# Moving the scaling of the float64 weights' lower words from VectorE to ScalarE

## The chip, the cores and the metric

The kernel runs on one core of a Trainium2 chip. The metric is the device time of one execution in microseconds, the median of several runs. Times inside an execution come from a hardware profile of one run; they count from the first instruction, and the distance from the first to the last instruction is called the span.

## The reference

Three layers follow one another: windowed attention (four heads plain, four dilated), a gated linear layer, and a soft mixture of experts. All arithmetic is on 2,304 tokens of 512 numbers.

```python
# attention: q, k, v are (4, 8, 576, 64); each row sees a window of 32 keys (heads 4-7: every 4th of 128)
scores = np.where(masks, scale * q @ k.T, -1e9)
attn = softmax(scores);  x = (attn @ v) -> (2304, 512)
# gated layer, w_gate and w_val are (512, 1536), w_out is (1536, 512)
x = (1 / (1 + np.exp(-(x @ w_gate))) * (x @ w_val)) @ w_out
# soft experts: phi (512, 32), w1 (8, 512, 1024), w2 (8, 1024, 512)
logits = x @ phi
slot_input = softmax(logits, axis=0).T @ x
slot_out = relu(slot_input @ w1) @ w2        # by expert, 4 slots each
out = softmax(logits, axis=1) @ slot_out
```

The inputs q, k, v, w1, w2 and phi are float32. The three weights of the gated layer arrive as float64 (numpy's `/ np.sqrt(...)` makes them so), and the kernel gets their raw 64-bit words. [...]

## The kernel before, in words

**Attention** is cut into 20 units, five token blocks n by four head pairs hp. A unit loads its q and k (line 269) and v (line 276), computes scores on TensorE (tile `s_ps`), a softmax (VectorE reductions and a subtraction, a ScalarE Exp at line 184, a normalization on VectorE in block 0 and on GpSimd in the others, line 189), is turned by TensorE transposes into `tr`, copied by ScalarE to `pt_ring` (line 196), and multiplied with v into `xp` (line 222; for later blocks it lies in the bank of `s_ps`). `finish_unit` splits that result into a high part `x_hi` (ScalarE cast, line 250) and a remainder `x_lo` (VectorE subtraction, line 251).

**The gated layer** runs `l1(n, f, ...)` for a token block n and 12 column groups f. Per f there are two products, gate and value, of 12 matmuls each into a bank `l1ps` (line 470; two banks): high weight by x_hi, high weight by x_lo, low weight by x_hi. ScalarE takes the gate's bank with a Tanh (line 480), VectorE the value's bank (line 456). The weights of an f come as `whl`: `split_w` casts them on ScalarE (line 433) and subtracts on VectorE or GpSimd (line 434). For block 0 and f = 0 to 11 the source of `whl` is the converted tile `fw` itself; in block 1 it is read back from DRAM (`wst`), where it was stored.

**The conversion** is the part that the change touches. `convert(z)` handles 18 tiles: 12 of gate and value weights, two per column group, and six of w_out (the last, by position, is number 17). `stage(z)` loads the raw words into `st` (line 361, one tile ahead, two buffers); `store()` writes an earlier result to DRAM (line 365). The conversion works in two halves of 128x512. For each half, four operations in this order: ScalarE turns the upper word to a scaled float (Prelu, line 379), VectorE shifts it by three bits (line 380), VectorE scales the lower word to a rounded integer (line 381), and GpSimd adds the two (line 382). So there are 36 of each. The first two conversions are written after step `C0 = 21` of block 0's attention, the others with `LA = 2` column groups of lead in the loop over f of block 0, and the six of w_out along block 1. After a w_out tile is converted, `slot_weights` turns and multiplies it on TensorE (line 408, tile `wt_ps`).

**What sets the order.** The program is written without waits. When it is built, a scheduler sets each engine's order: of the instructions that it takes to be ready, at times that it estimates, the one written earliest goes first, with line 480 and 456 preferred (`high_priority`) and with the order of some instructions kept as written (`keep_in_program_order`: most loads, TensorE's attention steps, the later pair products). On the chip each engine runs its own list in that order and stops at the first instruction whose inputs or buffer are not there. SP issues all the transfers that matter here, in one list: loads of q, k and v, `stage`, `store`, and the reloads of weights (line 898). Buffers are reused by tag: `st` has two, `whl` two, `fw` takes turns over four tags for the first 12.

After about 192 us there are no conversions any more: blocks 2 and 3 are computed as a pair, then block 4, and the experts.

Of the kernel before, what the change touches and what calls it, by code (L numbers as in the profile page):

```python
# [10 lines left out]
I32 = mybir.dt.int32  # L11
BF16 = mybir.dt.bfloat16
AF = mybir.ActivationFunctionType
ALU = mybir.AluOpType
# [42 lines left out]
def tile_kernel(  # L57
# [10 lines left out]
    nc = tc.nc  # L68
# [14 lines left out]
    def b8(tag, shape, dt, name):  # L83
        return big.tile(shape, dt, tag=tag, name=name, bufs=BUFS[tag])
# [272 lines left out]
    def stage(z):  # L357
        if z in staged:
            return
        staged[z] = b8("l2", [P, 1024, 2], U32, "st")  # L360
        ld(nc.sync.dma_start(staged[z].rearrange("p a b -> p (a b)"), wd[z].bitcast(U32)))

    def store():
        while stores:
            ld(nc.sync.dma_start(*stores.pop(0)))

    def convert(z):
        i = n_conv[0]
        n_conv[0] += 1
        stage(z)  # L370
        if i + 1 < len(turn):
            stage(turn[i + 1])
        st = staged[z]
        store()
        fw = b8(("ws", "ws", "gb", "xt")[i % 4] if i < NF else ("gb", "xt")[i % 2], [P, 2, 1024], F32, "fw")
        for h in range(2):
            c = slice(512 * h, 512 * h + 512)
            top, low = fw[:, 0, c], fw[:, 1, c]
            nc.scalar.activation(top, st[:, c, 1].bitcast(F32), AF.Prelu, scale=2.0**-112, alpha=2.0**32)  # L379
            nc.vector.tensor_scalar(top.bitcast(U32), top.bitcast(U32), 3, None, ALU.logical_shift_left)  # L380
            nc.vector.tensor_scalar(low.bitcast(I32), st[:, c, 0], 2.0**-29, None, ALU.mult)  # L381
            nc.gpsimd.tensor_tensor(low.bitcast(I32), top.bitcast(I32), low.bitcast(I32), ALU.add)  # L382
        if z < NF:
            stores.append((wg32[z // 2][:, z % 2], fw[:, 1]))
        else:
            y = z - NF
            stores.append((wo32[y // 2][:, 2 * (y % 2) : 2 * (y % 2) + 2].rearrange("p a c -> p (a c)"), fw[:, 1]))
            slot_weights(2 * y, fw[:, 1].rearrange("p (c x) -> p c x", c=2), 3)
        return fw[:, 1]
# [10 lines left out]
    def slot_weights(f, wo_f, lag):  # L400

        wt = pm.rearrange("p a b -> p (a b)").rearrange("p (k c x) -> p k c x", k=ND, c=2)
        at_ = {}

        def turned(c):
            wt_ps = ps_a.tile([P, ND, P], F32, tag="a", name="wt_ps")
            for kc in range(ND):
                nc.tensor.transpose(wt_ps[:, kc], wo_f[:, c, P * kc : P * kc + P], ident)
            nc.scalar.copy(wt[:, :, c], wt_ps)

        def product():
            pt_ps = ps_m.tile([P, 2, P], F32, tag="m", name="pt_ps")
            for kc in range(ND):
                nc.tensor.matmul(
                    pt_ps[32 * kc : 32 * kc + 32], lhsT=phi[:, kc, :], rhs=wt[:, kc], start=True, stop=True
                )
            at_["pt"] = cpool.tile([P, 2, P], F32, tag="pt", name="pt")
            nc.vector.tensor_copy(at_["pt"], pt_ps)

        def summed():  # L420
            wp_ps = ps_m.tile([P, 2, 32], F32, tag="m", name="wp_ps")
            for c in range(2):
                nc.tensor.matmul(wp_ps[:, c], lhsT=at_["pt"][:, c], rhs=i4, start=True, stop=True)
            nc.vector.tensor_scalar(wp[:, f : f + 2], wp_ps, 0.5, None, ALU.mult)

        for n, (step, *args) in enumerate(((turned, 0), (turned, 1), (product,), (summed,))):
            later.append((ticks[0] + lag + n, step, args))
# [453 lines left out]
    def ahead(z):  # L881
        if z < NF:
            conv[z] = convert(z)
# [34 lines left out]
    for f in range(NF):  # L918
        whl = split_w(wst[f // 2][:, f % 2])
        if f % 2:  # L920
            load_w(f // 2 + 2)
        l1(1, f, whl, beside)
        if NF + f in wo_at:
            convert(NF + wo_at[NF + f])
# [97 lines left out]
    for f in range(NF):  # L1022
        c = f % 4
# [255 lines left out]
```

## Time and profile before

| | |
|---|---|
| median of 3 runs | 497.39 us (496.50 to 498.11) |
| the profiled execution, its own time | 496.94 us |
| its span | 495.2 us |
| granted TensorE clock, mean | 0.992 |
| TensorE busy | 468.6 us, 95% of the span |
| VectorE busy | 311.0 us, 63% |
| ScalarE busy | 213.1 us, 43% |
| GpSimd busy | 156.8 us, 32% |

TensorE is busy nearly always, by the pipelined ends that the profile models. The shares are means over stages of different kinds, so they don't say what a change in one stage is worth. The rows below give the stages in which conversions run, and what TensorE waited for in them.

### The profile page before, as it was taken

The numbers are of one execution on the slowest core, as the hardware profiler recorded it, in microseconds if no ns is written. First come the engines' busy times: TensorE is split into PE (matmuls) and PEld (weight loads), VectorE is DVE, ScalarE is ACT, GpSimd is POOL, SyncE is SP. The second block draws the span as 40 slices with busy tenths as digits, with TensorE's granted clock in tenths as the row PEclk, the third lists the DMA queues.
The fourth block names the chain that finished last, engine by engine and source line by source line (L and its number), as shares of the span: only waits on it lengthen the run. The fifth ranks groups of instructions, "written<-read, shape, count | busy, mean of one in ns | idle before, by whom it ended". The sixth has DMA issues, their size and how long they took to land.

```text
span 495.2 us, 12830 instructions
## 1 busy us (share of the span) xinstructions
PE 468.6 (95%) x5488; PEld 357.3 (72%) x5488; DVE 311.0 (63%) x629; ACT 213.1 (43%) x414; POOL 156.8 (32%) x132
## 2 busy tenths in 40 slices
PE   6889999999899998999889999999999999999993
PEld 3558888887788876886557888888887889742552
DVE  3879898758666745436987656655547765541532
ACT  2455645435445534314744554554535343300223
POOL 0244536416445314235154323334212124110100
PEclk9899999999999999999999999999999999999998
DMA  8979978995896079120002201201499886579997
GB/s 301 421 276 361 351 234 306 310 344 195 322 368 253 2 253 394 63 86 1 1 1 86 85 25 61 86 5 80 142 372 422 345 326 259 190 296 367 428 402 239
DMA packets 23785, 112.14 MB, mean 226 GB/s; under 512 B 2352, under 2 KB 7216, under 8 KB 14640
## 3 DMA queue, kind: packets, MB, share of 16 engines
q1 hardware_dynamic: 23408, 111.06, 60.0%
q8 instruction: 43, 0.70, 0.6%
q10 hardware_dynamic: 320, 0.26, 0.2%
q14 instruction: 14, 0.11, 0.1%
HBM read 97.16 MB, written 14.16 MB: 225 GB/s over the span
## 4 chain that ended last, share of the span: by engine, by line
PE 80%; DVE 8%; DMA 4%; ACT 2%; issue 2%; POOL 1%; SPq 1%; DVEq 0%; ACTq 0%
PE l1ps L470 32%; PE pa L592 11%; PE pe L592 6%; PE tp L757 3%; PE s_ps L222 3%; PE h_ps L1045 3%; PE lt_ps L721 3%; PE pd L592 3%; PE s_ps L162 3%; PE so_ps L1104 3%; DMA wo<-fw 2%; PE sp L786 2%; PE tr L195 2%; DMA qk<-qkv 2%; DVE s L556 1%
## 5 line engine op out<-in xcount | busy, mean ns | idle before, releaser
L470 PE MATMUL l1ps<-x_hi,whl 128*128 128x512 f32 x384 | 129.4, 402 | 2.6 <-ACT x_hi L250 2.5
L470 PEld LDWEIGHTS l1ps<-x_hi,whl 128*128 128x128 f32 x384 | 71.7, 188 | 19.0 <-ACT x_hi L250 3.2
L470 PE MATMUL l1ps<-x_lo,whl 128*128 128x512 f32 x192 | 75.6, 394 | 0.0
L382 POOL TENSOR_TENSOR fw<-fw 128x512 int32<-128x512 int32 x36 | 49.0, 1370 | 61.7 <-DVE fw L381 24.7
L470 PEld LDWEIGHTS l1ps<-x_lo,whl 128*128 128x128 f32 x192 | 36.2, 188 | 6.6 <-DVE x_lo L251 0.2
L456 DVE SCALAR_TENSOR_TENSOR g<-g,l1ps 128x512 f32<-128x512 f32 (+1 forms) x36 | 21.4, 594 | 29.3 <-PE l1ps L470 29.0
L470 PE MATMUL l1ps<-x,whl 128*128 128x256 f32 x288 | 37.0, 285 | 0.0
L470 PEld LDWEIGHTS l1ps<-x,whl 128*128 128x128 f32 x288 | 35.4, 192 | 0.4 <-issue 0.2
L480 ACT ACTIVATE g<-l1ps 128x512 f32<-128x512 f32 (+1 forms) x36 | 18.9, 526 | 37.4 <-PE l1ps L470 37.4
L434 POOL TENSOR_TENSOR whl<-w,whl 128x512 fp32r<-128x512 f32 x12 | 15.9, 1326 | 51.2 <-ACT whl L433 39.7
L379 ACT ACTIVATE fw<-st 128x512 f32<-128x512 f32 x36 | 22.8, 675 | 12.4 <-DMA st<-wd 9.2
L757 PE MATMUL tp<-cst,g 128*128 128x128 f32 x216 | 28.0, 275 | 0.0
L757 PEld LDWEIGHTS tp<-cst,g 128*128 128x128 f32 x216 | 24.0, 140 | 5.0 <-issue 3.3
L762 ACT COPY gt<-tp 128x512 f32<-128x512 f32 x27 | 15.6, 584 | 25.0 <-PE tp L757 21.9
L176 DVE TENSOR_REDUCE mx<-s_ps 128x4 f32<-128x256 f32 x40 | 15.2, 413 | 14.3 <-PE s_ps L162 8.4
L380 DVE TENSOR_SCALAR fw<-fw 128x512 uint32<-128x512 uint32 x36 | 22.7, 640 | 1.9 <-ACT fw L379 1.0
L655 DVE TENSOR_TENSOR tm<-pe,tm 128x512 f32<-128x512 f32 x12 | 8.3, 691 | 24.1 <-PE pe L592 24.1
L434 DVE TENSOR_TENSOR whl<-fw,whl 128x512 fp32r<-128x512 f32 x24 | 20.9, 884 | 3.7 <-ACT whl L433 3.2
L381 DVE TENSOR_SCALAR fw<-st 128x512 int32<-128x512 uint32 x36 | 17.8, 528 | 7.7 <-DMA wst<-wg 3.7
L189 POOL TENSOR_TENSOR sm<-sm,su 128x512 f32<-128x512 f32 x12 | 13.6, 1130 | 28.3 <-DVE su L188 26.4
L434 POOL TENSOR_TENSOR whl<-wst,whl 128x512 fp32r<-128x512 f32 x12 | 15.9, 1326 | 19.0 <-ACT whl L433 11.7
L433 ACT CAST whl<-fw 128x512 fp32r<-128x512 f32 x24 | 14.6, 620 | 16.1 <-POOL fw L382 11.7
(455 smaller groups left out, 962.1 us busy)
## 6 DMA issues: line engine op xcount, KB each, us to landing
ew<-w SPq DMA_DIRECT2D x32, 1024.0 KB, 7.8
st<-wd SPq DMA_DIRECT2D x18, 1024.0 KB, 9.1
wst<-wg SPq DMA_DIRECT2D x12, 1024.0 KB, 7.7
v<-qkv SPq DMA_DIRECT2D x20, 512.0 KB, 6.1
wg<-fw SPq DMA_DIRECT2D x12, 512.0 KB, 7.8
w<-wg SPq DMA_DIRECT2D x6, 1024.0 KB, 7.5
qk<-qkv SPq DMA_DIRECT2D x10, 576.0 KB, 5.7
qk<-qkv SPq DMA_DIRECT2D x8, 528.0 KB, 5.5
```

The costliest lines, as they stand in the source:

```text
L176: nc.vector.tensor_reduce(mx[:, 4 * r : 4 * r + 4], u["s_ps"][r], AX.X, ALU.max)
L379: nc.scalar.activation(top, st[:, c, 1].bitcast(F32), AF.Prelu, scale=2.0**-112, alpha=2.0**32)
L380: nc.vector.tensor_scalar(top.bitcast(U32), top.bitcast(U32), 3, None, ALU.logical_shift_left)
L381: nc.vector.tensor_scalar(low.bitcast(I32), st[:, c, 0], 2.0**-29, None, ALU.mult)
L382: nc.gpsimd.tensor_tensor(low.bitcast(I32), top.bitcast(I32), low.bitcast(I32), ALU.add)
L434: (nc.gpsimd if pool[h] else nc.vector).tensor_tensor(whl[:, 1, h], src[:, h], whl[:, 0, h].bitcast(F32), ALU.subtract)
L456: return nc.vector.scalar_tensor_tensor(g, g, 1.0, val, ALU.add, ALU.mult)
L470: nc.tensor.matmul(pt[:, 0:nt], lhsT=whl[:, w_, a, dc, :], rhs=x_[n][:, dc, :], start=first, stop=(dc == HP_ORDER[-1] and w_ == 1),)
L480: nc.scalar.activation(g, pt[:, 0:nt], AF.Tanh, scale=0.5)
L592: nc.tensor.matmul(pt, lhsT=w[:, w_, P * c : P * c + P], rhs=x_[:, c], start=first and c == 0 and w_ == 0 and x_ is hi, stop=c == 1 and w_ ...
L757: nc.tensor.transpose(tp[:, c], g_sb[self.n, 4 * q + c][:, P * j : P * j + P], ident)
L762: nc.scalar.copy(to, tp)
```

## The change

One line in `convert`. The lower words of a half are multiplied by 2 to the power of -29 and written as rounded integers by a ScalarE activation with the function Copy and an immediate scale. Before, a VectorE operation did this. Inputs, output tile, shapes and everything around it are the same.

```diff
             top, low = fw[:, 0, c], fw[:, 1, c]
             nc.scalar.activation(top, st[:, c, 1].bitcast(F32), AF.Prelu, scale=2.0**-112, alpha=2.0**32)
             nc.vector.tensor_scalar(top.bitcast(U32), top.bitcast(U32), 3, None, ALU.logical_shift_left)
-            nc.vector.tensor_scalar(low.bitcast(I32), st[:, c, 0], 2.0**-29, None, ALU.mult)
+            nc.scalar.activation(low.bitcast(I32), st[:, c, 0], AF.Copy, scale=2.0**-29)
             nc.gpsimd.tensor_tensor(low.bitcast(I32), top.bitcast(I32), low.bitcast(I32), ALU.add)
```

## Rows read from the trace of the kernel before

**Rows 1.** Stretches: length, busy us (count) of PE, PEld, DVE, ACT, POOL; clock; DMA

```profile
15.00:36.00 21.00, 16.17 (x427) 11.67 (x426) 16.38 (x39) 12.30 (x25) 8.68 (x6) 0.97 0.91 357
36.00:120.00 84.00, 84.00 (x1161) 68.20 (x1162) 70.24 (x138) 42.71 (x80) 37.38 (x29) 1.00 0.84 296
120.00:192.00 72.00, 69.34 (x1191) 54.94 (x1189) 45.45 (x105) 34.45 (x67) 30.81 (x26) 1.00 0.71 256
```

**Rows 2.** TensorE's waits, 15 to 36 us: us in total, times, longest

```profile
PE l1ps L470 <- ACT x_hi L250: 2.5, 4, 1.2
PE xp L222 <- ACT pt_ring L196: 1.0, 2, 0.7
PE xp L222 <- issue: 0.7, 1, 0.7
PE tr L195 <- DVE x_lo L251: 0.6, 1, 0.6
```

**Rows 3.** TensorE's waits, 36 to 192 us

```profile
PE wt_ps L408 <- POOL fw L382: 1.4, 1, 1.4
PE s_ps L222 <- issue: 1.3, 1, 1.3
```

**Rows 4.** Groups: busy us, mean ns; then two lines: ns shortest/median/longest

```profile
L379 ACT ACTIVATE fw<-st 128x512 f32<-128x512 f32 x36 | 22.8, 675 | 12.4 <-DMA st<-wd 9.2
...
L381 DVE TENSOR_SCALAR fw<-st x36: 374/418/1516, 16.1 to 186.4; 128x512 int32<-128x512 uint32 x36
...
L434 DVE TENSOR_TENSOR whl<-fw,whl x24: 673/691/1787, 19.0 to 99.3; 128x512 fp32r<-128x512 f32 x24
```

**Rows 5.** ScalarE in order of time, 16 to 32 us (start us, us)

```profile
16.65 0.59 ACT L196 COPY pt_ring<-tr 128x512 f32<-128x512 f32 x1 [0.97 <-PE tr L195]
...
18.74 0.64 ACT L250 CAST x_hi<-xp 128x256 fp32r<-128x256 f32 x2
...
24.78 1.25 ACT L379 ACTIVATE fw<-st 128x512 f32<-128x512 f32 x2
26.15 0.59 ACT L196 COPY pt_ring<-tr 128x512 f32<-128x512 f32 x1
28.08 0.62 ACT L433 CAST whl<-fw 128x512 fp32r<-128x512 f32 x1 [1.34 <-POOL fw L382]
28.60 0.64 ACT L250 CAST x_hi<-xp 128x256 fp32r<-128x256 f32 x2
30.60 0.62 ACT L433 CAST whl<-fw 128x512 fp32r<-128x512 f32 x1 [1.35 <-POOL fw L382]
31.12 0.58 ACT L196 COPY pt_ring<-tr 128x512 f32<-128x512 f32 x1
```

**Rows 6.** VectorE in order of time, the same stretch

```profile
18.96 1.21 DVE L434 TENSOR_TENSOR whl<-fw,whl 128x512 fp32r<-128x512 f32 x1
20.10 0.74 DVE L251 TENSOR_TENSOR x_lo<-xp,x_hi 128x256 fp32r<-128x256 f32 x2
...
26.84 1.50 DVE L380 TENSOR_SCALAR fw<-fw 128x512 uint32<-128x512 uint32 x1
```

**Rows 7.** GpSimd in order of time, the same stretch

```profile
26.40 1.65 POOL L382 TENSOR_TENSOR fw<-fw 128x512 int32<-128x512 int32 x1 [6.77 <-DVE fw L381]
28.75 1.82 POOL L382 TENSOR_TENSOR fw<-fw 128x512 int32<-128x512 int32 x1 [0.70 <-DVE fw L381]
```

**Rows 8.** Three engines in order of time, 186 to 188 us

```profile
186.06 1.23 ACT L379 ACTIVATE fw<-st 128x512 f32<-128x512 f32 x2 [0.36 <-DMA wo<-fw]
186.08 0.76 DVE L381 TENSOR_SCALAR fw<-st 128x512 int32<-128x512 uint32 x2 [1.61 <-DMA wo<-fw]
...
187.09 0.75 DVE L380 TENSOR_SCALAR fw<-fw 128x512 uint32<-128x512 uint32 x2
...
187.59 2.61 POOL L382 TENSOR_TENSOR fw<-fw 128x512 int32<-128x512 int32 x2 [1.85 <-DVE fw L380]
```

**Rows 9.** SP's own waits, 15 to 192 us

```profile
SPq L361 <- DVE fw L381: 15.6, 4, 5.1
```

## The prediction

> **What bounds the kernel now.** Read first the busy times by stage [rows 1]. Half-words are converted from 15.0 us (first Prelu) to 189 us, and only there can the change act. That stretch falls in three: 15 to 36 us, where TensorE is busy 16.17 of 21; 36 to 120 us, where it is busy 84.00 of 84; 120 to 192 us, 69.34 of 72. In the middle stage VectorE is busy 70.24 of 84 and ScalarE 42.71: both have work all the time, and TensorE waits for neither, by the next two views.
>
> Read next what TensorE waited for. Up to 36 us: four waits for x_hi (2.5), two for pt_ring (1.0), one for x_lo (0.6), and 0.7 of issue, 4.8 in all [rows 2]. From 36 to 192 us: one wait of 1.4 for the last conversion's GpSimd add, and 1.3 of issue, in which it waited for nothing that the profile shows [rows 3]. So the conversions touch the end of the kernel in two places: the start, where the first block's attention has not yet filled TensorE's queue, and the last conversion, at 186 us. A change in the stretch cannot win more than these 7.5 us, and can lose only where cover runs out.
>
> **The prices.** The removed operation is line 381 on VectorE: 36 of them, median 418 ns, from 374 to 1516 [rows 4], so at least 36 x 0.42 = 15 us. Why some are long can be seen at the shift of line 380, the same kind of operation at the same size: at 26.84 us it took 1.50 [rows 6], and GpSimd's add ran from 26.40 to 28.05 [rows 7]. The added one is not in the trace with these types. Its nearest row is line 379, the Prelu: ScalarE, immediate scale, the same staging tile at the same stride, the same size, 675 ns on average [rows 4]; two in a row took 1.25 us at 24.78 [rows 5] and 1.23 at 186.06 [rows 8], so 0.62 each in a row. I take 0.62 in a row and 0.65 alone; the bounds are 0.58 (the pt_ring copy [rows 5]) and, as the price of an integer in and out is not shown, twice the Prelu, 1.3. So ScalarE gains 36 x 0.62 = 22 us and VectorE sheds 15 plus the stretches: the work costs 0.2 us more per piece on its new engine. The Trainium skill ("ScalarE: Activation LUTs", Rules for kernel authors) says to put a multiplication on VectorE rather than on ScalarE; 418 against 620 ns agrees, and if every piece lay on the path the rule would make 36 x 0.2 = 7 us of loss. It doesn't lie on the path in most places, by [rows 3]. No new table is needed: the same function, with a scale, already runs on ScalarE at the kernel's end (line 1117).
>
> **Stage 36 to 186 us: nothing.** At most 30 of the 36 pieces fall here. Were all in the middle stage, ScalarE would come to 42.71 + 30 x 0.62 = 61.3 of 84, 73% [rows 1]. The cover is the matmul queue, of which no wait but issue is left. Behind a ScalarE that runs late stand the tanh (which frees the l1 bank), pt_ring and x_hi; TensorE waits for these. If the cover were gone, each of the 15 conversions there would cost its pair, 1.25, 19 us together; nothing in [rows 3] is near it. The freed VectorE time (30 x 0.42) is worth nothing here, since TensorE never waits for VectorE.
> SP's queue: the load of the next staging tile (line 361) waits for the last reader of an old one, for line 381 15.6 us in 4 times [rows 9]; it will wait for the Copy. Behind it stand the loads of q, k and v, the stores and the reloads. It comes some tenths later or earlier, and no wait of TensorE in [rows 2, 3] is for a transfer. Nothing.
>
> **Start, conversion 0: +0.5.** ScalarE is idle 0.97 before pt_ring at 16.65 [rows 5], and the first Copy fits there. The second stands behind the second Prelu, ahead of the exp, the whl cast and the x_hi at 18.74, and pushes them by 0.62. The subtraction of line 434 at 18.96 (1.21) moves with the cast and so does the x_lo at 20.10 behind it [rows 6], for which TensorE already waits 0.6 [rows 2]. I take 0.5, as line 434's 1.21 is stretched (median of the line 0.69, longest 1.79 [rows 4]) and may shrink. Bounds: 0, when the order puts the second Copy behind x_hi; 1.2, when both stand ahead of pt_ring.
>
> **Start, conversion 1: +0.2.** Today: two Prelus at 24.78, pt_ring at 26.15, a cast of whl at 28.08 that waited 1.34 for the GpSimd add, x_hi at 28.60, a cast at 30.60 that waited 1.35, pt_ring at 31.12 [rows 5]. Two Copies in the group push pt_ring by 1.25 to 27.40. x_hi followed it by 2.45, 0.52 of them behind the cast, which now is done sooner: 27.40 + 1.93 = 29.33, 0.7 late. The way back: the second add started only at 28.75 and took 1.82 [rows 7], because its Copy stood behind the shift of 1.50. Now both Copies are there at 27.3 and the second add can end near 28.8, so the cast before the last pt_ring waits no more. x_hi to that pt_ring was 2.52, less the 0.52 behind the cast 2.0: 29.33 + 2.0 = 31.33 against 31.12. So 0.2 is left. Bounds: -0.6, when the Copies come behind pt_ring and the cast's wait goes anyway; +1.25, when nothing comes back.
>
> **End, conversion 17: -0.25.** The add starts at 187.59 after the shift at 187.09, which stands behind the two operations of line 381 [rows 8]. Now the shift can run when the first Prelu ends (186.06 + 0.65), and the Copy ends at 186.06 + 0.62 + 0.65 = 187.33: the add starts at 187.35, and TensorE's 1.4 [rows 3] becomes 1.15. If both Prelus come first, the Copy ends at 187.95, +0.36.
>
> **Sum.** 0.5 + 0.2 - 0.25 = +0.45 on the profiled execution's 496.94 us (span 495.2 and 1.74 around it), 497.39. The median of the runs is 0.45 above that execution, so 497.8. All bounds together: -0.9 to +2.8, that is 496.5 to 500.2.
>
> **The rivals.** Faster by over 0.3% is below 495.9, slower above 498.9; about 1.5 us is what a measurement of this kernel can tell from no change.
> *VectorE set the pace of the start.* It is busy 16.38 of 21 there, ScalarE 12.30 [rows 1]. Six pieces at 0.42 go, 2.5 us, and with them the stretches (1.50 against 0.42; 1.21 against 0.69). The Trainium skill ("GPSIMD Engine Reference", Key points) says that GpSimd shares its SBUF interfaces with VectorE and contends with some of its instructions; 374 against 1516 ns [rows 4] agrees. If the softmax and the subtractions come that much earlier, half of TensorE's 4.8 us could go: with -0.25 at the end, 497.4 - 2.65 = 494.7. Against it: 3.5 of the 4.8 are put down to ScalarE and 0.6 to VectorE [rows 2]. It decides from 1.5 us up. Chance 0.12.
> *ScalarE becomes the queue of the start.* The path there is a chain that goes TensorE, ScalarE, TensorE (pt_ring, x_hi, pt_ring), and the Copies stand ahead of it. With the upper bounds of conversions 0 and 1 (1.2, 1.25), the same 1.25 for conversion 2 ahead of the block's last x_hi, and nothing back: +3.7, 501.1; with a third of it back +2.5, 499.9. It decides when more than one of the three groups is not absorbed. For it: 3.5 of 4.8 us wait for ScalarE already [rows 2]. Against it: ScalarE still has 8.7 of 21 idle [rows 1]. Chance 0.20.
> *The order moves elsewhere.* The program's order on each engine is worked out from estimated times when it is built; a ScalarE with 36 more pieces can change places of other work, and 1.3 of issue [rows 3] can go or come again. Some 2 us either way, 495.4 or 499.4; chance 0.04.
> *The price is double.* Integers cost ScalarE 1.3 apiece: the two groups of the start are each 1.25 more, 0.6 more at the end, 499.9 to 500.9. Chance 0.04.
>
> **How the numbers follow.** The forecast, a loss of some tenths at the start and little else, has 0.60. Faster: 0.12 and half of 0.04, 0.14. Slower: 0.20, 0.04 and half of 0.04, 0.26. Same: 0.60. The predicted time is 497.8. The range is 495.7 to 500.0: it takes in all of the forecast's bounds but the last 0.2, the slower rival with a third back, and leaves out most of the faster one and the full slower one, under 2 in 10.
>
> **What will show it.** In the profile after: 36 ScalarE operations of 0.6 to 0.7 us on line 381; the longest shifts fewer; TensorE still at 84 of 84 in the middle stage; its waits for x_hi and pt_ring before 36 us between 3 and 5; the last add's wait near 1.15. I am wrong if TensorE waits for ScalarE after 40 us, if the waits before 36 us fall under 3.3 or pass 6.3, or if the Copy takes over 0.8 us.

## The result and the profile after

The change makes the kernel slower: 501.95 us median of 4 runs (501.64 to 502.53) against 497.74 of 4 runs of the kernel before (496.50 to 498.11), ratio 1.0088 with an interval of 1.0064 to 1.0111, so 4.2 us. The forecast was 497.8 and no measurable change; the time lies beyond the range, past the far end of the rival "ScalarE becomes the queue of the start".

The price of the new operation first. These are the groups of the two lines in the profile after: shortest, median and longest in ns.

```profile
L381 ACT ACTIVATE fw<-st x36: 644/666/699, 17.9 to 193.6; 128x512 int32<-128x512 uint32 x36
...
L380 DVE TENSOR_SCALAR fw<-fw x36: 375/461/1517, 16.6 to 193.7; 128x512 uint32<-128x512 uint32 x36
```

The Copy costs what its nearest row, the Prelu, costs (665 by the median in this profile); the integer types add nothing that shows. ScalarE is busy 231.7 us (before 213.1). VectorE has 300.5 (before 311.0): 10.5 less, where the 36 removed operations had taken 17.8 by their group in the profile before. Of the 7.3 between, 3.3 went into longer shifts: their group takes 26.0 where it took 22.7, a mean of 722 ns where it was 640, and 14 of the 36 took over 1 us, where 8 had. The other 4 are not traced.

The same three stretches as [rows 1], in the profile after (length, busy us and count of PE, PEld, DVE, ACT, POOL; clock; DMA):

```profile
15.00:36.00 21.00, 17.96 (x338) 13.39 (x336) 15.24 (x31) 12.92 (x26) 5.65 (x4) 0.68 0.94 343
36.00:120.00 84.00, 82.61 (x1122) 66.35 (x1115) 59.66 (x111) 52.25 (x99) 35.35 (x28) 0.98 0.80 287
120.00:192.00 72.00, 70.63 (x1310) 56.20 (x1309) 44.13 (x101) 38.45 (x76) 31.75 (x26) 1.00 0.66 238
```

In the first stretch TensorE is busy longer than before (17.96 against 16.17) with fewer matmuls (338 against 427). The clock column says why: 0.68 where it was 0.97. The middle stage lost 1.39 of its 84 us, and its clock reads 0.98.

What TensorE waited for in the profile after, 15 to 36 us (us in total, times, longest); it answers to [rows 2]:

```profile
PE l1ps L470 <- ACT x_hi L250: 2.4, 1, 2.4
PE xp L222 <- ACT pt_ring L196: 0.7, 1, 0.7
```

And from 36 to 200 us, beside [rows 3]:

```profile
PE s_ps L222 <- issue: 1.4, 2, 1.1
PE wt_ps L408 <- POOL fw L382: 1.0, 1, 1.0
PE l1ps L470 <- ACT x_hi L250: 0.9, 1, 0.9
PE l1ps L470 <- DVE x_lo L251: 0.5, 1, 0.5
```

Four waits for x_hi of 2.5 together became one of 2.4; two more, 1.4 together, fell just behind 36 us, and they are the middle stage's loss: the start now reaches into it. ScalarE around the one long wait, in order of time in the profile after (start us, us):

```profile
28.29 0.67 ACT L381 ACTIVATE fw<-st 128x512 int32<-128x512 uint32 x1
28.85 0.57 ACT L196 COPY pt_ring<-tr 128x512 f32<-128x512 f32 x1
30.44 0.62 ACT L433 CAST whl<-fw 128x512 fp32r<-128x512 f32 x1 [1.01 <-POOL fw L382]
32.13 0.62 ACT L433 CAST whl<-fw 128x512 fp32r<-128x512 f32 x1 [1.07 <-POOL fw L382]
32.65 0.64 ACT L250 CAST x_hi<-xp 128x256 fp32r<-128x256 f32 x2
34.56 0.59 ACT L196 COPY pt_ring<-tr 128x512 f32<-128x512 f32 x1 [1.26 <-PE tr L195]
```

This is the place of [rows 5], and the order is another. Before: pt_ring, cast, x_hi, cast, pt_ring. Now: pt_ring, cast, cast, x_hi, pt_ring. The second cast waits 1.07 for GpSimd's second add, and x_hi, which the next product needs, stands behind it though ScalarE is idle. When its input was there, TensorE's list of the profile after shows:

```profile
29.84 1.14 PE L222 MATMUL xp<-pt_ring,v 64*64 64x32 f32 x64
33.34 0.73 PE L470 MATMUL l1ps<-x_hi,whl 128*128 128x512 f32 x2 [2.37 <-ACT x_hi L250]
```

The input `xp` was ready at 29.84 + 1.14 = 30.98 and x_hi began at 32.65, 1.67 later. In the kernel before, `xp` was ready at 26.98 + 1.14 = 28.12 (its row stands with the second experiment) and x_hi began at 28.60 [rows 5], 0.48 later.

The end of the conversions, three engines in the profile after, the place of [rows 8]:

```profile
191.93 0.67 ACT L379 ACTIVATE fw<-st 128x512 f32<-128x512 f32 x1 [0.31 <-DMA wo<-fw]
...
192.50 0.65 ACT L381 ACTIVATE fw<-st 128x512 int32<-128x512 uint32 x1
...
193.23 1.28 POOL L382 TENSOR_TENSOR fw<-fw 128x512 int32<-128x512 int32 x1 [1.58 <-ACT fw L381]
...
194.56 0.66 PE L408 MATMUL wt_ps<-cst,fw 128*128 128x128 f32 x4 [1.01 <-POOL fw L382]
```

The add starts 1.30 after the first Prelu (before 1.53), and the wait is 1.0 instead of 1.4. Last, how late TensorE's same work stands against before: the first scores of block 1 at 40.07 (before 35.05, 5.0 late), the last operation of line 408, for w_out, starts at 196.9 (before 191.4, 5.5 late), the span is 500.8 (before 495.2, 5.6 late). What is lost is lost by about 40 us, and little is added behind it.

Not all of the 5.0 is lost at that wait. The third unit's `xp` starts at 29.84 where it started at 26.98, so 2.9 are there ahead of it, in the long stretch at the low clock. And behind the wait the clock fell a second time in this execution:

```profile
38.00:40.00 2.00, 1.53 (x5) 0.50 (x4) 0.58 (x2) 0.28 (x1) 1.27 (x1) 0.71 0.00 0
40.00:42.00 2.00, 2.00 (x67) 1.66 (x67) 0.73 (x2) 0.32 (x1) 0.00 (x0) 0.50 0.00 0
```

The first scores of block 1 stand there and took 1.18 us instead of 0.86.

### The profile page after: what moved, and what is told of

It reads as the page before. It is cut to its first block, busy times and chain, and to the rows that moved or that the text cites. A ratio compares the mean times of both kernels' runs of the same rounds, so it can differ in the third digit from the quotient of the medians.

```text
span 500.8 us, 12850 instructions
## 1 busy us (share of the span) xinstructions
PE 473.2 (95%) x5483; PEld 361.5 (72%) x5488; DVE 300.5 (60%) x593; ACT 231.7 (46%) x450; POOL 156.2 (31%) x132
## 4 chain that ended last, share of the span: by engine, by line
PE 81%; DVE 7%; DMA 4%; ACT 3%; issue 1%; POOL 1%; SPq 1%; DVEq 0%; ACTq 0%; POOLq 0%
PE l1ps L470 32%; PE pa L592 11%; PE pe L592 6%; PE tp L757 3%; PE s_ps L162 3%; PE s_ps L222 3%; PE h_ps L1045 3%; PE lt_ps L721 3%; PE pd L592 3%; PE so_ps L1104 2%; DMA qk<-qkv 2%; DMA wo<-fw 2%; PE tr L195 2%; PE sp L786 2%; PE xp L222 1%
## 5 line engine op out<-in xcount | busy, mean ns | idle before, releaser
L470 PE MATMUL l1ps<-x_lo,whl 128*128 128x512 f32 x192 | 76.7, 400 | 0.5 <-DVE x_lo L251 0.5
L382 POOL TENSOR_TENSOR fw<-fw 128x512 int32<-128x512 int32 x36 | 47.6, 1323 | 72.8 <-ACT fw L381 52.5
L380 DVE TENSOR_SCALAR fw<-fw 128x512 uint32<-128x512 uint32 x36 | 26.0, 722 | 22.1 <-ACT fw L379 22.0
L456 DVE SCALAR_TENSOR_TENSOR g<-g,l1ps 128x512 f32<-128x512 f32 (+1 forms) x36 | 21.4, 595 | 28.8 <-PE l1ps L470 28.7
L379 ACT ACTIVATE fw<-st 128x512 f32<-128x512 f32 x36 | 24.0, 665 | 13.2 <-DMA st<-wd 9.1
L762 ACT COPY gt<-tp 128x512 f32<-128x512 f32 x27 | 15.6, 584 | 25.0 <-PE tp L757 21.9
L381 ACT ACTIVATE fw<-st 128x512 int32<-128x512 uint32 x36 | 24.0, 666 | 0.0
L162 PE MATMUL s_ps<-qk 64*32 64x64 f32 x1280 | 18.5, 237 | 3.6 <-DMA qk<-qkv 3.6
```

The source lines that it names most:

```text
L162: nc.tensor.matmul(u["s_ps"][r][32 * i : 32 * i + 32, t, :], lhsT=q[64 * r : 64 * r + 64, 128 * t + 32 * i : 128 * t + 32 * i + 32], rhs=k ...
L381: nc.scalar.activation(low.bitcast(I32), st[:, c, 0], AF.Copy, scale=2.0**-29)
L456: return nc.vector.scalar_tensor_tensor(g, g, 1.0, val, ALU.add, ALU.mult)
L470: nc.tensor.matmul(pt[:, 0:nt], lhsT=whl[:, w_, a, dc, :], rhs=x_[n][:, dc, :], start=first, stop=(dc == HP_ORDER[-1] and w_ == 1),)
```

## The experiments

Expectations were written before each run. In the first four kernels only some conversions use ScalarE, by one condition on the conversion's number (`i`, in `convert`), here for `late`:

```diff
-            nc.scalar.activation(low.bitcast(I32), st[:, c, 0], AF.Copy, scale=2.0**-29)
+            nc.scalar.activation(low.bitcast(I32), st[:, c, 0], AF.Copy, scale=2.0**-29) if i >= 3 else nc.vector.tensor_scalar(low.bitcast(I32), st[:, c, 0], 2.0**-29, None, ALU.mult)
```

**late: conversions 3 to 17 on ScalarE.**

> Copies on ScalarE from conversion 3 on, VectorE for conversions 0 to 2. Theory A (ScalarE's queue in the first 40 us is the whole loss): TensorE's order and the first 40 us are those of the kernel before, so the time is within 0.3% of it, 496.3 to 499.2. Theory B (the load of 30 Copies on ScalarE in the middle stages costs): at least 2 us of the 4.2 stay, 500 or more. Theory C (TensorE's lower granted clock from 11 to 28 us came from a late transfer of q and k and has nothing to do with the change): the time follows the clock of the start, not the kernel.

Measured: 498.04 against 497.92, ratio 0.9999 (0.9968 to 1.0031). Thirty of the 36 operations, moved, cost nothing and bring nothing that 0.3% can show. TensorE's order is that of before, and ScalarE's in the start is pt_ring, cast, x_hi, cast, pt_ring again. The third unit's `xp` and x_hi in `late`:

```profile
28.79 1.17 PE L222 MATMUL xp<-pt_ring,v 64*64 64x32 f32 x64
...
30.02 0.65 ACT L250 CAST x_hi<-xp 128x256 fp32r<-128x256 f32 x2 [0.99 <-PE xp L222]
```

This `xp` starts 1.8 later than before, behind work at a lower clock (0.50 for some 3 us around 27 us), and the first scores of block 1 come at 36.05, only 1.0 late. Keep the two numbers for the next run, in which `xp` starts sooner and the scores come later.

**early: conversions 0 to 2 on ScalarE (`i < 3`).**

> Copies on ScalarE for conversions 0 to 2 only, VectorE for the other 15. Theory A: the whole loss, 501 to 503. Theory B: under 500. Theory C: follows the clock of the start.

Measured: 502.79, ratio 1.0118 (1.0052 to 1.0184). The whole loss comes from six operations. The profile of `early` is the better one to read: up to 27 us it goes with the kernel before (the first `xp` starts at 17.29 in both; clock 0.83 from 10 to 20 us in both, 1.00 from 20 to 30). In the profile of the kernel after, the scores that wait for the third transfer of q and k, issued before any conversion, began at 12.27, after TensorE had stood still for 2.98 us; before, the first nine of them began at 11.19 after 1.41, the other 55 at 12.10. The lower level came sooner there and stayed until about 28 us. In `early` it had ended by 17 us, and the whole loss is there: the long low stretch of the start is not needed for it. ScalarE in order of time in `early`:

```profile
18.80 0.62 ACT L250 CAST x_hi<-xp 128x256 fp32r<-128x256 f32 x2
19.32 0.67 ACT L381 ACTIVATE fw<-st 128x512 int32<-128x512 uint32 x1
...
27.53 0.57 ACT L196 COPY pt_ring<-tr 128x512 f32<-128x512 f32 x1
29.13 0.62 ACT L433 CAST whl<-fw 128x512 fp32r<-128x512 f32 x1 [1.02 <-POOL fw L382]
30.82 0.62 ACT L433 CAST whl<-fw 128x512 fp32r<-128x512 f32 x1 [1.07 <-POOL fw L382]
31.34 0.64 ACT L250 CAST x_hi<-xp 128x256 fp32r<-128x256 f32 x2
33.25 0.59 ACT L196 COPY pt_ring<-tr 128x512 f32<-128x512 f32 x1 [1.26 <-PE tr L195]
```

The same swap stands there. The third unit's `xp` starts at 28.16, ahead of that of `late` (28.79), and yet x_hi comes 1.3 later than there and the first scores of block 1 come 3.7 later. Step by step against the forecast (start times in us; the first four rows are ScalarE's, by [rows 5] for before):

| | before | early | shift | forecast |
|---|---|---|---|---|
| first unit's x_hi | 18.74 | 18.80 | 0.06 | 0.5 |
| third pt_ring | 26.15 | 27.53 | 1.38 | 1.25 |
| third unit's x_hi | 28.60 | 31.34 | 2.74 | 0.7 |
| fourth pt_ring | 31.12 | 33.25 | 2.13 | 0.2 |
| first scores of block 1 (TensorE) | 35.05 | 39.73 | 4.68 | - |

The last row adds 2.55 to the one above it, for the same work. TensorE's list in `early` between the two:

```profile
32.04 0.74 PE L470 MATMUL l1ps<-x_hi,whl 128*128 128x512 f32 x2 [2.75 <-ACT x_hi L250]
...
34.59 1.94 PE L222 MATMUL xp<-pt_ring,v 64*64 64x32 f32 x64
37.27 1.22 PE L470 MATMUL l1ps<-x_hi,whl 128*128 128x512 f32 x2 [0.75 <-ACT x_hi L250]
...
39.73 1.06 PE L162 MATMUL s_ps<-qk 64*32 64x64 f32 x64
```

The same in the kernel before, with the third unit's `xp` ahead of it:

```profile
26.98 1.14 PE L222 MATMUL xp<-pt_ring,v 64*64 64x32 f32 x64
...
31.75 1.14 PE L222 MATMUL xp<-pt_ring,v 64*64 64x32 f32 x64 [0.35 <-ACT pt_ring L196]
33.64 0.73 PE L470 MATMUL l1ps<-x_hi,whl 128*128 128x512 f32 x2 [0.75 <-ACT x_hi L250]
...
35.05 0.86 PE L162 MATMUL s_ps<-qk 64*32 64x64 f32 x64
```

The wait for x_hi between them is the same 0.75. The 64 matmuls of `xp` took 1.94 instead of 1.14, and the way from the product to the scores 2.46 (37.27 to 39.73) instead of 1.41: 0.80 and 1.05 us, with no wait in them. The clock column explains it; windows of 2 us in `early`:

```profile
30.00:32.00 2.00, 0.00 (x0) 0.00 (x0) 1.86 (x2) 1.17 (x3) 0.79 (x1) 1.00 0.99 340
32.00:34.00 2.00, 1.96 (x9) 1.54 (x10) 0.83 (x3) 0.75 (x2) 0.00 (x0) 0.85 0.83 330
34.00:36.00 2.00, 2.00 (x55) 1.42 (x56) 0.87 (x2) 1.52 (x3) 0.96 (x1) 0.50 0.29 111
...
38.00:40.00 2.00, 2.00 (x30) 0.97 (x36) 0.00 (x0) 0.60 (x1) 1.14 (x1) 0.50 0.00 0
```

TensorE does nothing from 30 to 32 us, inside the wait of 2.75; then the granted clock falls to 0.50, the lower level (1.2 GHz), until about 40 us. The kernel before reads 1.00 in each of the five windows from 30 to 40 us. In this execution, then, 2.1 us of the 4.7 come from order and waits, and 1.85 of the other 2.55 are the same matmuls at the lower level; 0.7 is the later start of `xp`, behind products that ran partly at it. Some of the delay is made good later: the last operation of line 408 starts at 195.2, 3.8 late.

**only0 and only1: one conversion of the start alone (`i == 0`, `i == 1`).**

> Copies on ScalarE for conversion 0 only. By the order of the instructions, TensorE already has its first block in the order of the changed kernel here, and ScalarE has both casts of whl ahead of the third x_hi. Theory A, if the second cast ahead of that x_hi (1.6 us) and the later first l1 matmul (3 us) carry the loss: 2 to 4 us slower than before. If the four conversion operations in a row ahead of the third pt_ring carry it: under 1.5 us.

> Copies on ScalarE for conversion 1 only; TensorE's order is that of the kernel before. Theory A, if the four operations in a row ahead of the third pt_ring (1.25 us) and the second cast ahead of the third x_hi (1.6 us) carry the loss: 2 to 3 us slower. If conversion 0 carries it: under 1.5 us.

Measured: only0 502.90, ratio 1.0091 (1.0056 to 1.0126); only1 501.16, ratio 1.0076 (1.0043 to 1.0108). Either of them brings nearly the whole loss, more than was expected of either, so the parts do not add. In `only0` nothing is added to ScalarE at conversion 1, and yet ScalarE's list there reads:

```profile
28.17 0.62 ACT L433 CAST whl<-fw 128x512 fp32r<-128x512 f32 x1 [0.60 <-POOL fw L382]
30.80 0.62 ACT L433 CAST whl<-fw 128x512 fp32r<-128x512 f32 x1 [2.01 <-POOL fw L382]
31.33 0.64 ACT L250 CAST x_hi<-xp 128x256 fp32r<-128x256 f32 x2
```

Both casts again ahead of x_hi, with ScalarE idle 2.01 between them. The load on ScalarE cannot be the cause at this place; the order can. In `only1` TensorE's order is that of before and ScalarE's has the swap. Part of the loss of these two lies elsewhere. Their first scores of block 1 are 3.0 and 4.5 late, but the last operation of line 408 is 6.2 and 9.3 late (the profiled execution of `only1`, 506.13 us, is its longest). Their last conversion makes TensorE wait 2.2 and 2.4 for GpSimd (before 1.4 [rows 3]), which is 0.8 and 1.0 of that; the rest is not traced.

**chain_first: the kernel after, with the chain of block 0 preferred on ScalarE.**

```diff
-        nc.scalar.copy(pt_ring[:, u["z"] % 4].rearrange("p c i q -> p c (i q)"), tr)
+        with tc.high_priority(offset=HIP if u["id"][0] == 0 else 0): nc.scalar.copy(pt_ring[:, u["z"] % 4].rearrange("p c i q -> p c (i q)"), tr)
...
-            nc.scalar.copy(hi, xp[y])
+            with tc.high_priority(offset=HIP if n == 0 else 0): nc.scalar.copy(hi, xp[y])
```

> All 36 Copies on ScalarE as in the change, but block 0's pt_ring copies and x_hi casts are preferred by the scheduler, so that ScalarE's order puts the third pt_ring ahead of three of conversion 1's four operations and the third x_hi between the two casts of whl, as before the change. Theory order (the loss comes from where the third pt_ring and x_hi stand in ScalarE's list): at least two thirds come back, 499.5 or less. Theory price (the Copies' own time on ScalarE in the first 40 us is the loss, wherever they stand): 501 or more.

Measured: 499.08 against 497.96, ratio 1.0026 (1.0001 to 1.0050). All 36 Copies stay on ScalarE and about 3 of the 4.2 us come back. ScalarE in order of time:

```profile
26.18 0.59 ACT L196 COPY pt_ring<-tr 128x512 f32<-128x512 f32 x1
...
29.23 0.62 ACT L433 CAST whl<-fw 128x512 fp32r<-128x512 f32 x1 [0.77 <-POOL fw L382]
29.76 0.64 ACT L250 CAST x_hi<-xp 128x256 fp32r<-128x256 f32 x2
30.95 0.62 ACT L433 CAST whl<-fw 128x512 fp32r<-128x512 f32 x1 [0.55 <-POOL fw L382]
```

pt_ring stands at 26.18 (before 26.15) and x_hi between the casts again. TensorE, which waited 2.4 for this x_hi in the kernel after and 1.2 before, does not wait for it at all: from 28 to 34 us its profile shows no wait. That is not ScalarE's list alone. TensorE's list changed with the preference too: of the ten products of line 470 between the second and the third unit's `xp` in the kernel after, three now stand behind the third and fill the time until x_hi is there. So this run shows what the chain's preference is worth on both engines together.

**before_wait: the kernel before, with the wait alone.** VectorE keeps line 381. The third unit's x_hi is multiplied by a tile of ones that GpSimd writes right after conversion 1's second add, so it must wait for that add as in the kernel after.

```diff
-            nc.scalar.copy(hi, xp[y])
+            nc.scalar.activation(hi, xp[y], AF.Copy, scale=one[0][:, 0:1]) if (n, hp) == (0, HP_ORDER[2]) else nc.scalar.copy(hi, xp[y])
...
-            nc.gpsimd.tensor_tensor(low.bitcast(I32), top.bitcast(I32), low.bitcast(I32), ALU.add)
+            nc.gpsimd.tensor_tensor(low.bitcast(I32), top.bitcast(I32), low.bitcast(I32), ALU.add); (nc.gpsimd.tensor_scalar(one[0], low[:, 511:512], 0.0, 1.0, ALU.mult, ALU.add) if (i, h) == (1, 1) else None)
```

> The kernel before, no Copy of the conversions on ScalarE; only the third x_hi is scaled by a column of ones that GpSimd writes after conversion 1's second add, so that it can't start before that add and ScalarE has both casts of whl ahead of it. TensorE's order is unchanged. Theory order: TensorE's wait for x_hi grows by 1.5 to 2.5 us, and the time by 1.5 to 4 (the wait, and a lower clock after it): 499.5 to 502. Theory price: within 1 us of the kernel before.

Measured: 504.65 against 497.96, ratio 1.0142 (1.0105 to 1.0178). ScalarE and TensorE's wait for it:

```profile
31.20 0.62 ACT L433 CAST whl<-fw 128x512 fp32r<-128x512 f32 x1 [1.88 <-POOL fw L382]
31.73 0.83 ACT L250 ACTIVATE x_hi<-xp,one 128x256 fp32r<-128x256 f32 x2
...
32.62 1.22 PE L470 MATMUL l1ps<-x_hi,whl 128*128 128x512 f32 x2 [2.32 <-ACT x_hi L250]
```

Without a single operation moved, and with TensorE's order unchanged, one x_hi behind GpSimd's second add costs more than the change did. The third unit's `xp` starts at 29.16 here, much as in `late` (28.79), which lost nothing. It is more than was expected, and why it exceeds the change is open: the first scores of block 1 are 4.5 late here (39.6), much as in `early` (4.7), in an execution that at 502.77 us is among the shortest of its six. A small part is the edit's own: this x_hi takes 0.83 us where the others take 0.64.

**The clock: after_fill, before_fill, late_fill, chain_fill.** Five more idle matmuls (of zeros, into a bank that nobody reads; the kernel before has some already) are put ahead of the third unit's scores, where TensorE waits for its transfer; all other orders stay as they were.

```diff
-            scores(us[z], ts)
+            keep_warm(5 if head and z == 2 and 0 in ts else 0); scores(us[z], ts)
```

> The changed kernel with five more idle matmuls (about 1.1 us) ahead of the scores of the third unit, where TensorE waits for q and k; all other orders are the same. Theory clock (the granted clock falls after TensorE's idle time there, and a lower clock costs time): the clock stays at its upper level through 17 us in the profile and the kernel gains 0.5 to 2, to 500 to 501.5, but stays over 1.5 slower than before, as the waits for x_hi remain. If the clock costs nothing: 501.5 to 502.5.

> The kernel before with the same five idle matmuls. Theory clock: gains 0.3 to 1.5, to 496.5 to 497.6, and the runs spread less. If the clock costs nothing, or the transfer comes too early for the filling: 497.9 or up to 0.5 more.

> Copies on ScalarE from conversion 3 on, and the five idle matmuls ahead of the third unit's scores. If the middle stages are as indifferent to the change as the run with the first three conversions on VectorE said, this is the kernel before with the filling: 496.5 to 497.9. If the unloaded VectorE is worth something once the start is in order: under 496.5.

> The changed kernel with pt_ring and x_hi of block 0 preferred and the five idle matmuls. If the order of ScalarE's list and the clock after TensorE's idle time are two separate losses, their cures add: 499.1 less 0.7 to 1.6, that is 497.5 to 498.4, no longer slower than before by over 0.3%. If they are one loss: 499 or more.

Measured: after_fill 500.37, ratio to before 1.0049 (1.0033 to 1.0065; without the five matmuls 1.0088); before_fill 497.19, 0.9984 (0.9958 to 1.0009); late_fill 497.84, 0.9992 (0.9976 to 1.0008); chain_fill, the edit of chain_first and the five matmuls together on the kernel after, 497.87 against 497.92, 0.9999 (0.9980 to 1.0018). On the kernel after they win back some 1.6 us (501.95 to 500.37; the two intervals just touch) with no order changed, on the kernel before nothing that can be told from zero. The first stretches of the kernel after and of after_fill, in this order in the two fences:

```profile
10.00:20.00 10.00, 6.72 (x147) 4.69 (x152) 5.45 (x15) 3.52 (x6) 1.28 (x1) 0.58 1.02 421
20.00:30.00 10.00, 10.00 (x162) 7.51 (x160) 8.79 (x20) 6.79 (x14) 2.70 (x2) 0.57 0.95 321
```

```profile
10.00:20.00 10.00, 6.10 (x194) 4.17 (x193) 6.41 (x18) 4.35 (x9) 1.28 (x1) 0.91 1.02 421
20.00:30.00 10.00, 9.67 (x126) 7.23 (x130) 8.41 (x18) 5.88 (x12) 3.08 (x2) 0.57 0.94 346
```

The clock from 10 to 20 us rises from 0.58 to 0.91, but the lower level still comes behind it. That the better clock makes the 1.6 us is likely and not shown: in the two profiles only 0.6 of it stands at the first scores of block 1 (39.43 against 40.07). And a low clock ahead of the third unit's `xp` can cost next to nothing: in the profile of before_fill it reads 0.52 from 20 to 30 us, and the last operation of line 408 starts at 191.6, where it started at 191.4 before. With the order mended and the idle matmuls in, the change costs nothing. No version is measurably better than the kernel before.

## Why the prediction was wrong

**The step that failed** is "Start, conversion 1: +0.2". It took ScalarE's list to stay cast, x_hi, cast, and x_hi to be late only by the Copies ahead of pt_ring, 0.7. It assumed more: that the cast ahead of x_hi would be "done sooner", and that the cast behind it "waits no more", since the second add "can end near 28.8". Neither held. In `early` the first cast began at 29.13 (before 28.08), waiting 1.02 for GpSimd's first add. The second add needs the second shift, and in the kernel after that shift still took 1.51 beside GpSimd's first add (1.84 at 28.57), so the second add ran only from 30.83. A late second add behind x_hi costs less: chain_first has it there, its cast waits 0.55, and the loss is 1.1. But the list was worked out anew with the Copies in it, and the second cast went ahead of x_hi; an engine that runs its list in order then waits for GpSimd with the chain's next step behind it. By `early`, x_hi came 2.74 late instead of 0.7, and the last pt_ring 2.13 instead of 0.2. The forecast's way back (2.0 from x_hi to the next pt_ring, before 2.52) did happen, 1.91 in `early`, but behind a later x_hi. chain_first puts x_hi back between the casts and loses only 1.1 (499.08 less 497.96); before_wait makes the wait without the change and loses more than the change. TensorE's own new order is not needed for the loss: only1 and before_wait keep the old one.

**What was missing from the sum** is TensorE's clock. Each wait was priced by its length. In `early` the 2.75 us in which TensorE stood still were followed by nearly 7 us at the lower level, in which identical work took 1.85 longer; before, with no stop as long there, the clock stayed at 1.00. after_fill points the same way without showing it: 1.6 us come back with matmuls that compute nothing. How the 4.2 us of the median divide between waits and clock stays open. The profiled execution of the kernel after has most of its lower level ahead of the wait (clock 0.58 and 0.57 in the windows above) and some 3 us of it behind (38 to 42 us), and the mean clock of the runs does not settle it: late_fill's runs have a mean of 0.987 and the time of before, whose mean in the same series is 0.990; the kernel after has 0.981.

**Conversion 0, +0.5**, came out at its lower bound in `early`: the second Copy stands behind x_hi, which moved by 0.06. Yet only0 shows that moving these two operations costs 0.9% by itself, with the new orders that come with it, TensorE's too: the transpose of the second unit now stands ahead of the first product of line 470. The prediction had "The order moves elsewhere" as a rival with 0.04 and some 2 us; that was the mechanism, at the place and in the direction of the rival "ScalarE becomes the queue of the start", whose own reason (too much work on ScalarE ahead of the chain) is not what only0 and before_wait show.

**What was right.** The price, 0.666 against the 0.62 to 0.65 taken; the doubled price is out. The middle stage is worth nothing that can be measured in either direction: `late` moves 30 of 36 and gives 0.9999, and in its profile TensorE is busy 84.00 of the 84 us with ScalarE at 52.96, so VectorE's freed time buys nothing and ScalarE is still covered. The profile after alone, with 82.61 instead of 84.00, would have misled here; its loss sits in two waits just behind 36 us. The end, -0.25: the add came 0.23 sooner and the wait fell from 1.4 to 1.0. SP's queue waits 18.1 for line 381 instead of 15.6 [rows 9], and no wait of TensorE answers to it.

Of the signs that the prediction named, three failed. "The longest shifts fewer" did not come: 14 took over 1 us instead of 8. The second shift now runs right behind its Prelu and meets the first add, as at 36 us in the profile after: Prelu to 36.84, add from 36.37, shift from 36.88 for 1.04. TensorE is not at 84 of 84 in the middle stage. And its waits before 36 us are 3.1, under the 3.3 below which the prediction called itself wrong, but only because 1.4 of them moved just behind 36 us, where they make the 82.61.

The Trainium skill's rule ("ScalarE: Activation LUTs", Rules for kernel authors) that a multiplication belongs on VectorE gave the right direction. By the medians it would make 36 x (666 - 418) ns = 8.9 us if every operation lay on the path; `late` shows that 30 of them cost nothing, and the loss of the other six came with the order, not with the price.

## What to carry to other kernels

Before moving work onto an engine that has time to spare, read that engine's list around the chain that sets the end: an operation of the chain behind one that waits for a third engine waits with it, however idle the engine is. Where a scheduler makes the list, moved work changes it, also at places where nothing was added; give the chain's operations preference there, or expect the order to be another. And price a wait of TensorE in the start not by its length alone: look at the granted clock in the microseconds behind it.

## What the runs showed of the hardware that was not expected

A ScalarE Copy with 32-bit integers in and out costs what a float Prelu of the same size costs: 666 ns against 665 in the profile after. VectorE's shift of 128x512 took 0.42 us alone (the one at 28.00 in the profile after) and 1.50 to 1.51 beside a GpSimd add, at the same place before, after, in early, in chain_first and in before_wait; the Trainium skill ("GPSIMD Engine Reference", Key points) names the contention for the shared SBUF interfaces, and these numbers show its form. The long shift has no length of its own: it ends 0.28 to 0.30 us after the add that it met, in each of these five runs (in the profile after, the add ends at 28.57 + 1.84 = 30.41 and the shift at 29.18 + 1.51 = 30.69). So what the shift loses is about the part of the add that is left when the shift starts. The same kernel's runs spread with the mean granted clock: the kernel before took 495.5 us to 500.8 us in one series of 22 runs, at mean clocks from 0.983 to 0.994.
